# Order of the stores and of the key and value loads in part 1 of a memory-attention and SwiGLU kernel

## The chip, the core and the metric

The kernel runs on one core of a Trainium2 chip. The core has a matrix engine (PE, with its weight loads shown as PEld), a vector engine (DVE), a scalar engine (ACT), a general engine (POOL) and a sync engine (SP) whose queue issues the DMAs here. The metric is the device time of one launch in microseconds; lower is better. The time before is the median of three runs.

## The reference

Inputs: `q`, `k`, `v` of shape (8 batches, 8 heads, 576, 64), `phi` of shape (8, 8, 576, 32), and float64 weights `w_gate`, `w_val` (512 x 1536), `w_out` (1536 x 512) and `rms_g` (512).

```python
a = exp(phi - max(phi, axis=2));  a = a / (sum(a, axis=2) + 1e-9)      # softmax over the 576 positions
k_m = einsum('bhsm,bhsd->bhmd', a, k)                                  # 32 memory slots per head
v_m = einsum('bhsm,bhsd->bhmd', a, v)
attn = softmax(q @ k_m^T / 8)                                          # 576 x 32
x = (attn @ v_m) as 4608 tokens x 512
xn = x / sqrt(mean(x*x) + 1e-6) * rms_g
out = (silu(xn @ w_gate) * (xn @ w_val)) @ w_out                       # 4608 x 512
```

## The kernel before

Part 1 makes, for each batch b, the small matrices k_m and v_m, and for the first four batches also the attention weights. Part 2 is the gated network, in 48 steps `i` (two passes over 12 slices of the 1536 hidden columns, with two pairs of batches in each pass); into its first pass the attention of the other four batches is woven (`attend_steps`, `x2`).

Part 1 for one batch b: `load_phi` loads phi, `prep` takes its maximum and exponential into `e_bd` (lines 562 to 605) and adds some of its chunks on POOL into `es` (L617, L619; how many is `ESN[b]`). `load_kv(b, hp)` loads k and v of one pair of heads. `kv_steps(b)` has six chunks of matmuls (`kvp`, L636): the first three, the first half, need head pairs 0 and 1, the last three, the second half, need head pairs 2 and 3. Then come `sums` (matmuls with a column of ones, L651; `es` shortens them), `post1` (DVE, L659 to L668), `turn` (PE, L680), `post2` (ACT, and `vg` on POOL at L701), `self_products` (L710) and `post3` (`gram`, L719). For batches 4 to 7 `store` writes `vg` to `vg_dram` (L726) and, for 5 and 7, `gram` to `gram_dram` (L729); part 2 reads them back (`vgl<-vgd`, L1096, and `gb<-gd`, L199).

The key and value tiles of batches 2, 5 and 7 share the four buffers of the tag `kv`; those of 0, 3, 1, 4 and 6 lie in places that part 2 uses later (`kv_0x`, `kv_1x`). A load into a buffer waits on SP for the last reader of the tile that was there.

The float64 weights arrive as raw words (`raw`, two buffers) and are split into float32 parts by `convert` on DVE, ACT and POOL (L389 to L453); the results of slices are also written to DRAM (`wd<-wh`, `wd<-wl`, L464, and `od`, L459) and read back in the second pass by `reload` (L477). The first two slices (n = 0 and 1) are converted in part 1.

`x_steps` turns and normalises the attention weights of a pair of batches: `tp`, `xp`, then the chain `m`, `rinv` on DVE (L296 to L313), `rp` on PE (L230), `at` on DVE (L238), `ath` and `atl` (L258, L259).

Order. All steps of a part go into a list `ev` of (time, function) pairs, the times being in the planner's units, from the table `PRM`; the list is sorted and the functions are called in that order. The framework's scheduler then walks a modelled time line: of the instructions that its model holds to be ready, the earliest in the list goes first. So an instruction that waits, by the model, can be passed by a later one. On the chip each engine and the SP queue run what they got strictly in order. `load` ties each load behind the one issued before it (`issue_after`), so loads stay in the order of the list among themselves; stores and part 2's transfers have no such tie. The time of a key and value load in the list is

```python
ev.append((K_AT[b] + PRM["KD"][b * HP + hp], lambda b=b, hp=hp: load_kv(b, hp)))
```

which gives 101.115 for head pair 0 of batch 7 (167.28 - 66.165), and 109.651, 107.591, 113.281 and 111.017 for head pairs 0 to 3 of batch 5 (121.436 less the four values). The raw weights of slice 0 have 111.332 (`CV`).

Of the kernel before, what the change touches and what calls it, by code (L numbers as in the profile page):

```python
# [8 lines left out]
F32 = mybir.dt.float32  # L9
# [9 lines left out]
XTTR = True  # L19
WB = 4  # L20
PRM = dict(
    DS=150,
    KB=4,
    QB=3,
    K_AT=[13.363, 15.05, 40.982, 64.708, 100.72, 121.436, 147.13, 167.28],
    KP=0.88,
    POST=[-0.317, -0.206, 4.032, 7.881, 15.383, 23.226],
    P1=4.084,
    PREP=[4.511, 5.867, 6.271, 6.307, 20.4],
    PD=[1.603, 10.918, 5.724, 18.42, 6.909, 0.895],  # L30
    EXP=[-9.517, 14.262, 1.741, 4.567, 14.552, 4.082],
    ES=1.541,
    PH=[9.097, 16.192, 41.396, 73.222, 103.794, 133.428],
# [30 lines left out]
    O=[0.116, 0.297, 0.452, 0.514, 0.874, 0.991, 1.365, 1.487, 1.518],
    PRE=[-0.635, 0.045, 0.27, 1.342, 2.044, 2.566],
    PRE0=[-0.813, 0.784, 1.109, 1.622, 2.25, 2.293],
    PI=0.13,
    PSW=[1.981, 2.035, 1.951, 2.415, 3.159, 3.803],
    SU=[1.877, 3.104, 5.776, 6.56, 9.726, 12.211, 13.413, 15.536],
    AO=[0.214, 0.237, 0.237, 0.276, 0.397, 0.423, 0.543, 0.581, 0.621, 0.621, 0.621, 0.819, 1.065, 1.397],  # L70
    XB=[17.199, 22.761],
    XS=[0.1086, 0.0359],
    XM=[22.138, 25.161],
    XN=[-0.302, -0.244, -0.092, 0.028, 0.161, 0.484, 0.518, 0.593, 0.603],
    LV=[20.282, 20.03, 20.406, 21.652],
# [26 lines left out]
def kernel(  # L102
# [25 lines left out]
    nc = tc.nc  # L128
# [3 lines left out]
    HP = H // 2  # L132
# [6 lines left out]
    G = 2  # L139
# [190 lines left out]
    issued = []  # L330
# [4 lines left out]
            issued.append(nc.sync.dma_start(out, in_).ins)  # L335
# [42 lines left out]
    def convert(kind, n):  # L378

        d = {}  # L380
        nm = f"{kind}_{n}"
        V = nc.vector

        def s0():
            d["raw"] = t = raw.pop((kind, n))
            hw = t[:, :, 1]
            d["ex"] = ex = wp[0].tile([P, 512], I32, tag="ex", name=f"ex{nm}")
            with behind():
                V.tensor_scalar(out=ex, in0=hw, scalar1=0x7FF00000, scalar2=None, op0=ALU.bitwise_and)  # L389
# [9 lines left out]

        def s1():  # L400
            ex = d["ex"]
            if not ((kind < 2 and n < 2 and PRM["CA"]) or ((kind == 2 or n >= 2) and PRM["CB"])):
# [7 lines left out]

        def s2():
            d["m"] = m = wp[0].tile([P, 512], I32, tag="mi", name=f"mi{nm}")
            with behind():
                V.tensor_scalar(
                    out=m, in0=d["raw"][:, :, 1], scalar1=0xFFFFF, scalar2=None, op0=ALU.bitwise_and
                )
            mf = m.bitcast(F32)
            with behind():
                V.scalar_tensor_tensor(  # L419
                    out=mf, in0=d["raw"].bitcast(U32)[:, :, 0], scalar=2.0 ** -32, in1=m,  # L420
                    op0=ALU.mult, op1=ALU.add,
                )

        def s3():
            mf = d["m"].bitcast(F32)
            nc.scalar.activation(mf, mf, AF.Copy, scale=2.0 ** -20, bias=1.0)  # L426
            if kind < 2 and n < 2:
                d["w"] = wp[0].tile([P, 512], F32, tag="w", name=f"w{nm}")
            else:
                d["w"] = sb.tile([P, 512], F32, tag="w2", name=f"w{nm}", bufs=WB)  # L430

        def s4():
            m, ex = d["m"].bitcast(F32), d["ex"].bitcast(F32)
            on_pool = kind == 2 or n >= 2 or PRM["CE"][n] & (1 << kind)
            (nc.gpsimd if on_pool else V).tensor_tensor(out=d["w"], in0=m, in1=ex, op=ALU.mult)  # L435

        def s5():
            w = d["w"]
            if kind == 2:
                dh = wp[1].tile([P, 512], F32R, tag="oh", name=f"oh{n}", bufs=2)  # L440
                dl = wp[1].tile([P, 512], F32R, tag="ol", name=f"ol{n}", bufs=2)
                wosplit[n] = dh, dl
                src = w
            else:
                if kind == 0:
                    wsplit[n] = (
                        wp[n % 2].tile([P, HP, 2, P], F32R, tag="wh", name=f"wh{n}"),
                        wp[n % 2].tile([P, HP, 2, P], F32R, tag="wl", name=f"wl{n}"),
                    )
                dh, dl = (x[:, :, kind, :] for x in wsplit[n])  # L450
                src = w.rearrange("p (hp f) -> p hp f", hp=HP)
            nc.scalar.copy(dh, src)
            nc.gpsimd.tensor_tensor(out=dl, in0=src, in1=dh.bitcast(F32), op=ALU.subtract)  # L453

        def s6():

            if kind == 2:
                for a, t in enumerate(wosplit[n]):
                    nc.sync.dma_start(o_dram[n][:, a], t.bitcast(F32))  # L459
            elif kind == 1:  # L460
                for a, t in enumerate(wsplit[n]):
                    for h in range(2):
                        r = 64 * (h ^ a)
                        nc.sync.dma_start(w_dram[n][r:r + 64, h], t[64 * h:64 * h + 64].bitcast(F32))  # L464
# [15 lines left out]
    with ExitStack() as c1:  # L480
# [33 lines left out]
        st = {}  # L514
# [110 lines left out]
        def kv_steps(b):  # L625
# [97 lines left out]
                    split_v(b, st.pop(("vg", b)))  # L723

            def store():
                nc.sync.dma_start(vg_dram[b], st.pop(("vg", b)))  # L726
# [544 lines left out]
```

## Time and profile before

| what | value |
|---|---|
| time, median of 3 runs | 876.38 us (875.77 to 877.84) |
| time of the profiled execution | 876.4 us |
| its span, first to last instruction | 874.6 us |
| PE busy | 826.1 us (94%) |
| DVE, ACT, POOL busy | 541.1, 398.4, 315.3 us |
| mean granted PE clock | 0.982 |
| part 2's first matmuls (`vp`, L981) | 133.6 us after the start |

Rows of a timeline give start, duration, engine, line, operation and tiles, how many instructions are merged, and in brackets the idle time before them with what ended it. Rows of a table by windows give, for each stretch, its length and then busy time (and count) of PE, PEld, DVE, ACT and POOL, the granted PE clock (1.00 is full), the DMA engines' busy share and GB/s. Rows of the waits give the total, how many, and the longest. Matmul ends are modelled, so back-to-back matmuls overlap in the rows; their pace is the merged duration over the count. A float32 matmul appears as two rows.

### The profile page before, as it was taken

Reading aid. Unit: us, or ns where it says so; the run is one execution under the profiler, and the core shown is the slowest. Engines: PE = TensorE matmul, PEld = TensorE weight load, DVE = VectorE, ACT = ScalarE, POOL = GpSimd, SP = SyncE. Lnnn points to the kernel's source line nnn. Section 1 sums busy time; section 2 is a strip of 40 time slices with the busy share of each in tenths; the row PEclk is TensorE's granted clock in tenths of the full one; section 3 lists DMA queues with packets and bytes.
Section 4 is the critical chain, followed back from the end, with each engine's and each line's share of the span. In section 5 each row is a group of like instructions: output and inputs, shape, how many; then the busy total and the mean of one; then the engine's idle time right before and its main releaser. Section 6 shows DMA issues by size and latency. Waiting matters only on the chain.

```text
span 874.6 us, 16472 instructions
## 1 busy us (share of the span) xinstructions
PE 826.1 (94%) x6191; PEld 737.7 (84%) x6191; DVE 541.1 (62%) x985; ACT 398.4 (46%) x712; POOL 315.3 (36%) x268
## 2 busy tenths in 40 slices
PE   4998798989999999999999999989999999999997
PEld 4887777979988988978989977968999998999996
DVE  6679666878569888798889637402444444444434
ACT  3666336767655556646555413334322323232220
POOL 2475425644443553543534612302211212122120
PEclk9999797999999999999999999999999999999999
DMA  8992916553343453532543455755645546453437
GB/s 324 364 388 60 329 62 155 138 151 113 125 120 103 130 153 100 159 113 97 149 137 117 142 133 112 199 154 133 175 92 164 137 123 175 107 144 80 97 97 168
DMA packets 110246, 131.64 MB, mean 151 GB/s; under 512 B 45140, under 2 KB 74840, under 8 KB 110168
## 3 DMA queue, kind: packets, MB, share of 16 engines
q1 hardware_dynamic: 110168, 130.60, 52.2%
q8 instruction: 49, 0.80, 0.4%
q14 instruction: 29, 0.24, 0.1%
HBM read 73.93 MB, written 31.46 MB: 120 GB/s over the span
## 4 chain that ended last, share of the span: by engine, by line
PE 71%; DVE 11%; DMA 5%; issue 4%; ACT 4%; POOL 3%; SPq 2%; POOLq 0%; ACTq 0%; DVEq 0%
PE po L1064 28%; PE pg L1017 14%; PE pv L1017 14%; PE vp L981 3%; PE vq L931 3%; PE kvp L636 2%; DMA q<-in_q_dram 1%; DVE ex L389 1%; POOL w L435 1%; PE kvp L651 1%; DVE mi L419 1%; DVE acc L1072 1%; POOL hl L1045 1%; DVE ex L392 1%; DVE xl L994 1%
## 5 line engine op out<-in xcount | busy, mean ns | idle before, releaser
L1045 POOL TENSOR_TENSOR hl<-hf,hh 128x512 fp32r<-128x512 f32 (+1 forms) x86 | 126.3, 1471 | 280.9 <-ACT hh L1044 278.7
L1072 DVE TENSOR_TENSOR acc<-po,acc 128x512 f32<-128x512 f32 x180 | 123.2, 688 | 121.2 <-PE po L1064 120.2
L1064 PE MATMUL po<-oh,hh 128*128 128x512 f32 x387 | 155.8, 405 | 12.0 <-DVE acc L1072 4.0
L1064 PE MATMUL po<-ol,hh 128*128 128x512 f32 x387 | 153.8, 397 | 2.1 <-DMA ol<-od 2.1
L1064 PE MATMUL po<-oh,hl 128*128 128x512 f32 x387 | 153.3, 396 | 0.0
L1026 DVE TENSOR_TENSOR hf<-pv,sg 128x256 f32<-128x256 f32 x192 | 84.7, 452 | 101.1 <-PE pv L1017 52.7
L1025 ACT ACTIVATE sg<-pg 128x256 f32<-128x256 f32 x192 | 76.8, 410 | 129.1 <-PE pg L1017 121.4
L1064 PEld LDWEIGHTS po<-oh,hh 128*128 128x128 f32 x387 | 72.8, 189 | 27.4 <-DVE acc L1072 6.2
L1017 PE MATMUL pg<-ath,xh 128*128 128x320 f32 (+1 forms) x384 | 87.4, 301 | 4.6 <-ACT xh L993 4.4
L1017 PE MATMUL pg<-ath,xl 128*128 128x320 f32 (+1 forms) x384 | 86.4, 298 | 1.0 <-DMA xl<-sl 1.0
L1064 PEld LDWEIGHTS po<-oh,hl 128*128 128x128 f32 x387 | 73.2, 189 | 16.6
L1017 PE MATMUL pv<-ath,xl 128*128 128x320 f32 (+1 forms) x384 | 86.1, 297 | 0.0
L1017 PE MATMUL pv<-ath,xh 128*128 128x320 f32 (+1 forms) x384 | 85.7, 299 | 0.2 <-DVE hf L1026 0.2
L1017 PE MATMUL pg<-atl,xh 128*128 128x320 f32 (+1 forms) x384 | 84.7, 296 | 0.0
L1017 PE MATMUL pv<-atl,xh 128*128 128x320 f32 (+1 forms) x384 | 84.3, 297 | 0.0
L1044 ACT CAST hh<-hf 128x512 fp32r<-128x512 f32 (+1 forms) x86 | 57.4, 672 | 57.4 <-DVE hf L1026 41.0
L1064 PEld LDWEIGHTS po<-ol,hh 128*128 128x128 f32 x387 | 73.3, 189 | 11.9 <-DMA ol<-od 2.9
L435 POOL TENSOR_TENSOR w<-mi,ex 128x512 f32<-128x512 f32 x35 | 45.1, 1289 | 95.2 <-ACT mi L426 65.4
L1017 PEld LDWEIGHTS pg<-ath,xh 128*128 128x128 f32 x384 | 64.5, 189 | 10.0 <-ACT xh L993 5.2
L994 DVE TENSOR_TENSOR xl<-vp,xh 64x1024 fp32r<-64x1024 f32 x48 | 58.5, 1218 | 21.5 <-ACT xh L993 20.8
L1017 PEld LDWEIGHTS pg<-ath,xl 128*128 128x128 f32 x384 | 64.3, 190 | 4.1 <-issue 1.4
L1017 PEld LDWEIGHTS pv<-ath,xh 128*128 128x128 f32 x384 | 63.3, 190 | 3.3 <-PE pg L1017 0.4
(150 smaller groups left out, 1525.0 us busy)
## 6 DMA issues: line engine op xcount, KB each, us to landing
xh<-sh SPq DMA_DIRECT2D x192, 64.0 KB, 2.1
xl<-sl SPq DMA_DIRECT2D x192, 64.0 KB, 2.0
out_dram<-acc SPq DMA_DIRECT2D x72, 128.0 KB, 2.4
raw<-in_moe_w_gate_dram SPq DMA_DIRECT2D x12, 512.0 KB, 4.1
raw<-in_moe_w_val_dram SPq DMA_DIRECT2D x12, 512.0 KB, 3.8
wd<-wh SPq DMA_DIRECT2D x24, 256.0 KB, 3.2
wd<-wl SPq DMA_DIRECT2D x24, 256.0 KB, 3.7
raw<-in_moe_w_out_dram SPq DMA_DIRECT2D x12, 512.0 KB, 3.6
```

Of the source, the lines that this page charges most:

```text
L435: (nc.gpsimd if on_pool else V).tensor_tensor(out=d["w"], in0=m, in1=ex, op=ALU.mult)
L636: nc.tensor.matmul(kvp[64 * par:64 * par + 64, cc, 0:128], e_bd[j][:, hp, c, :], st["kv", b, hp][:, :, 64 * c:64 * c + 64], start=(c == 0) ...
L931: nc.tensor.matmul(vp[:, h, e, :], vall[a][:, cc, k:k + 4, :].rearrange("p q m -> p (q m)"), w, start=(a == 0), stop=(a == 1),)
L981: nc.tensor.matmul(vp[:, cc, e, :], lhs(l), r[:, 2 * cc + e, :], start=(n == 0), stop=(n == 2),)
L994: urgent.append(nc.vector.tensor_tensor(out=xl[rows], in0=src, in1=xh[rows].bitcast(F32), op=ALU.subtract).ins)
L1017: nc.tensor.matmul(pt[:, :N], l[cc][:, b, half * P:half * P + P], r[:, cc, b, t0:t0 + n, :].rearrange("p t x -> p (t x)"), start=(m == 0), ...
L1025: nc.scalar.activation(sg[:, :N], pg[:, :N], AF.Silu)
L1026: urgent.append(nc.vector.tensor_tensor(out=hf[:, :, b, :], in0=pv[:, :N].rearrange("p (t x) -> p t x", x=64), in1=sg[:, :N].rearrange("p ...
L1044: nc.scalar.copy(hh, hv)
L1045: nc.gpsimd.tensor_tensor(out=hl, in0=hv, in1=hh.bitcast(F32), op=ALU.subtract)
L1064: nc.tensor.matmul(po, l[:, tt, :], r, start=(m == 0), stop=(m == 5))
L1072: nc.vector.tensor_tensor(out=accs[key], in0=po, in1=accs[key], op=ALU.add).ins
```

## The change

`store_behind` ties a store behind the last load handed out so far. It is used for the stores of `vg` and `gram` (L726, L729) and for the stores of the converted slices 0 and 1 (L464). With a new number `LK` of 150, no key or value load has a time above 149.9 in the list, and no store of `vg` or `gram` one below 150. Most of the other numbers of `PRM` are new as well. Of the diff, the table is cut to the entries that are discussed later and some neighbours:

```diff
-    DS=150,
+    LK=150,
+    DS=154.273,
-    K_AT=[13.363, 15.05, 40.982, 64.708, 100.72, 121.436, 147.13, 167.28],
-    KP=0.88,
+    K_AT=[13.363, 15.05, 40.982, 64.708, 100.72, 121.436, 147.13, 167.903],
+    KP=0.914,
...
-    KD=[-15.069, -115.131, -42.204, -7.345, -6.094, -15.243, -0.175, -2.835, -28.265, -16.354, -17.024,
+    KD=[-15.069, -115.131, -42.204, -7.345, -6.094, -15.243, -0.175, -2.835, -29.404, -16.354, -17.024,
         -8.311, -12.025, -12.235, -27.337, -21.619, -22.801, -22.01, -23.715, -24.999, -11.785, -13.845,
-        -8.155, -10.419, -16.375, -22.685, -11.543, -19.501, -66.165, -9.755, -3.349, -20.028],
+        -8.155, -10.419, -16.375, -22.685, -11.543, -19.501, -20, -9.755, -3.349, -20.028],
...
-    QE=[4, 0],
-    CE=[3, 2],
-    XE=[12, 11, 29, 21],
-    ESN=[2, 3, 2, 0, 3, 1, 1, 1],
+    QE=[0, 0],
+    CE=[3, 0],
+    XE=[12, 11, 23, 29],
+    ESN=[2, 3, 2, 2, 3, 1, 1, 1],
...
-    VD=[29.86, 23.48, 21.637, 34.098],
+    VD=[29.894, 23.48, 16.936, 31.545],
...
-    RL=[-1.906, -3.752, -5.714],
-    RW=[1.932, 0.552],
+    RL=[-1.906, -3.412, -5.53],
+    RW=[1.622, 0.859],
...
+    def store_behind(out, in_):
+
+        with tc.issue_after(issued[-1]):
+            nc.sync.dma_start(out, in_)
...
-                        nc.sync.dma_start(w_dram[n][r:r + 64, h], t[64 * h:64 * h + 64].bitcast(F32))
+                        (store_behind if n < 2 else nc.sync.dma_start)(
+                            w_dram[n][r:r + 64, h], t[64 * h:64 * h + 64].bitcast(F32)
+                        )
...
             def store():
-                nc.sync.dma_start(vg_dram[b], st.pop(("vg", b)))
+                store_behind(vg_dram[b], st.pop(("vg", b)))
                 if j:
                     pr = b // 2
-                    nc.sync.dma_start(gram_dram[pr], gram[pr])
+                    store_behind(gram_dram[pr], gram[pr])
...
-                ev.append((K_AT[b] + 6 * PRM["KP"] + PRM["POST"][5] + PRM["VD"][b - 2 * G], store))
+                ev.append((max(K_AT[b] + 6 * PRM["KP"] + PRM["POST"][5] + PRM["VD"][b - 2 * G], PRM["LK"]), store))
...
-                    ev.append((K_AT[b] + PRM["KD"][b * HP + hp], lambda b=b, hp=hp: load_kv(b, hp)))
+                    ev.append((min(K_AT[b] + PRM["KD"][b * HP + hp], PRM["LK"] - 0.1), lambda b=b, hp=hp: load_kv(b, hp)))
```

`ESN[3]` of 2 instead of 0 lets POOL add two pairs of chunks of batch 3 ahead of its sums. `CE`, `QE` and `XE` say for single operations which engine takes them: the product of slice 1's second half goes from POOL to DVE, the last copies of the first four turned queries from DVE to ACT, and of the copies in `x_steps` for the later pairs one goes from DVE to ACT and one changes place. The other entries of the table that are not shown shift times in the list by mostly under half a unit in part 2 and by up to a few units in part 1.

More of the change, by code (lines that the diff above doesn't have):

```diff
@@ L21 @@
 PRM = dict(
-    DS=150,
+    LK=150,
+    DS=154.273,
     KB=4,
     QB=3,
-    K_AT=[13.363, 15.05, 40.982, 64.708, 100.72, 121.436, 147.13, 167.28],
-    KP=0.88,
[L27 to L33, printed above, removed]
+    K_AT=[13.363, 15.05, 40.982, 64.708, 100.72, 121.436, 147.13, 167.903],
+    KP=0.914,
+    POST=[0.041, 0.041, 3.361, 8.581, 15.173, 23.226],
+    P1=4.425,
+    PREP=[4.511, 6.478, 6.478, 6.478, 20.4],
+    PD=[1.603, 10.918, 5.603, 17.822, 6.909, 0.895],
+    EXP=[-7.764, 14.262, 1.692, 4.567, 14.552, 4.761],
+    ES=1.262,
+    PH=[9.097, 16.336, 41.396, 73.222, 103.794, 133.428],
     S_AT=[32.949, 48.182, 51.299, 66.888, 103.621, 110.401, 116.081, 122.952],
-    KD=[-15.069, -115.131, -42.204, -7.345, -6.094, -15.243, -0.175, -2.835, -28.265, -16.354, -17.024,
+    KD=[-15.069, -115.131, -42.204, -7.345, -6.094, -15.243, -0.175, -2.835, -29.404, -16.354, -17.024,
         -8.311, -12.025, -12.235, -27.337, -21.619, -22.801, -22.01, -23.715, -24.999, -11.785, -13.845,
-        -8.155, -10.419, -16.375, -22.685, -11.543, -19.501, -66.165, -9.755, -3.349, -20.028],
-    QD=[7.122, 5.589, 2.612, 8.893, 23.53, 19.934, 25.06, 15.038],
-    PD0=1.045,
+        -8.155, -10.419, -16.375, -22.685, -11.543, -19.501, -20, -9.755, -3.349, -20.028],
+    QD=[9.78, 5.589, 2.612, 12.908, 23.53, 19.934, 25.06, 15.038],
+    PD0=0.952,
     QL=3.761,
-    OL=3.513,
-    QO=[-1.164, 3.407, -1.815, -0.482, 0.012, 2.591],
-    SO=[7.743, 14.98, 18.206, 24.112],
+    OL=3.483,
+    QO=[-0.964, 4.247, -1.615, 1.156, 0.212, 3.193],
+    SO=[7.875, 14.417, 17.251, 24.624],
     X_AT=[100.536, 150.686],
-    XP=1.796,
+    XP=2.099,
     LAG=0.891,
@@ L49 @@
     CV2=160.133,
-    CP2=1.09,
-    QE=[4, 0],
-    CE=[3, 2],
-    XE=[12, 11, 29, 21],
-    ESN=[2, 3, 2, 0, 3, 1, 1, 1],
+    CP2=1.098,
+    QE=[0, 0],
+    CE=[3, 0],
+    XE=[12, 11, 23, 29],
+    ESN=[2, 3, 2, 2, 3, 1, 1, 1],
     SUM=[2, 2, 1, 0, 0, 1, 2, 1],
@@ L59 @@
     RS=6.461,
-    RP=0.555,
-    GV=[0.232, 0.246, 0.274, 0.752, 0.884, 1.089],
+    RP=0.036,
+    GV=[0.232, 0.246, 0.295, 0.762, 0.884, 1.143],
     VW=[-0.104, -0.023, 0.07],
     VW0=0.373,
[L64 to L70, printed above, removed]
-    XB=[17.199, 22.761],
[L72 to L75, printed above, removed]
-    VD=[29.86, 23.48, 21.637, 34.098],
-    U=[[-1.581, -1.578, -1.37, -1.197, -0.96, -0.96], [-1.522, -1.522, -1.12, -1.12, -1.036, -0.964], [-1.618,
-        -1.5, -1.335, -1.003, -1.003, -0.071]],
-    RL=[-1.906, -3.752, -5.714],
-    RW=[1.932, 0.552],
+    O=[0.116, 0.266, 0.452, 0.514, 0.874, 0.991, 1.365, 1.487, 1.518],
+    PRE=[-0.635, 0.045, 0.28, 1.342, 2.044, 2.566],
+    PRE0=[-0.813, 0.786, 1.109, 1.622, 2.25, 2.437],
+    PI=0.14,
+    PSW=[1.697, 2.033, 1.739, 2.203, 2.947, 3.543],
+    SU=[1.877, 3.104, 5.776, 6.56, 9.726, 12.952, 13.928, 15.536],
+    AO=[0.214, 0.215, 0.237, 0.276, 0.397, 0.423, 0.543, 0.581, 0.621, 0.621, 0.621, 0.819, 1.069, 1.397],
+    XB=[17.199, 22.761],
+    XS=[0.1086, 0.034],
+    XM=[22.138, 25.107],
+    XN=[-0.264, -0.206, -0.075, 0.066, 0.199, 0.522, 0.635, 0.635, 0.641],
+    LV=[20.329, 20.215, 20.555, 21.814],
+    VD=[29.894, 23.48, 16.936, 31.545],
+    U=[[-1.358, -1.358, -1.358, -1.197, -0.96, -0.832], [-1.522, -1.522, -1.12, -1.12, -1.036, -1.036],
+        [-1.54, -1.422, -1.257, -0.925, -0.925, 0.007]],
+    RL=[-1.906, -3.412, -5.53],
+    RW=[1.622, 0.859],
     CB=1,
```

## The prediction

> **What bounds the kernel now.** I read the busy times by window first, to see where PE is not full. (Columns: window, its length, busy time and count of PE, PEld, DVE, ACT, POOL, then granted clock, DMA share, GB/s.)
>
> ```profile
> 61.00:85.50 24.50, 22.78 (x344) 18.36 (x341) 23.15 (x56) 16.17 (x30) 11.15 (x11) 1.00 0.31 107
> 85.50:92.70 7.20, 1.84 (x11) 1.07 (x10) 5.21 (x17) 3.98 (x6) 4.87 (x9) 0.77 0.94 248
> 92.70:100.00 7.30, 7.26 (x99) 7.08 (x100) 2.35 (x2) 1.31 (x3) 1.42 (x2) 0.73 1.06 398
> 100.00:112.70 12.70, 11.22 (x183) 10.08 (x181) 11.77 (x27) 5.58 (x12) 7.68 (x9) 0.88 0.76 276
> 139.80:540.00 400.20, 386.20 (x2632) 346.75 (x2633) 310.52 (x526) 224.96 (x387) 177.49 (x137) 1.00 0.46 129
> 540.00:600.00 60.00, 55.99 (x327) 49.24 (x326) 17.12 (x30) 23.58 (x47) 16.72 (x13) 0.97 0.59 153
> 600.00:875.00 275.00, 268.93 (x1608) 242.76 (x1607) 116.65 (x200) 78.35 (x154) 54.94 (x39) 1.00 0.52 131
> ```
>
> Part 2 is PE's: it idles 14.0 us of 400 in the first pass, 4.0 around 570 and 6.1 later. Part 1 has one hole: from 85.5 to 92.7 PE works 1.84 of 7.2 us, while DVE, full before (23.15 of 24.5), has a little work and then none. The chain of waits says what ended it:
>
> ```profile
> 86.23 0.85 SPq L335
> 87.12 5.57 DMA kv<-in_v_dram
> 92.74 3.62 PE kvp L636 x33
> ```
>
> The chain runs through a key and value load that SP issued late. Why late is in SP's timeline, read against the list's times:
>
> ```profile
> 53.08 0.45 SPq L335 DMA_DIRECT2D kv<-in_k_dram  x1
> ...
> 58.69 0.33 SPq L335 DMA_DIRECT2D kv<-in_k_dram  x1
> ...
> 61.81 0.38 SPq L335 DMA_DIRECT2D raw<-in_moe_w_val_dram  x1
> 78.14 0.34 SPq L726 DMA_DIRECT2D vgd<-vg  x1
> 84.19 1.15 SPq L464 DMA_DIRECT2D wd<-wh  x2
> 85.60 0.45 SPq L464 DMA_DIRECT2D wd<-wl  x1
> 86.14 0.94 SPq L335 DMA_DIRECT2D kv<-in_k_dram  x1
> ```
>
> Loads go in the order of the list. By its times the four from 53.08 to 58.69 (two are left out) are batch 7's head pair 0 (101.115), then batch 5's 1, 0 and 3; the raw weights (111.332) follow, and batch 5's head pair 2 (113.281) is the one at 86.14. The tag has four buffers, and the early tile of batch 7 holds one that batch 5 needs. PE and DVE show the loop:
>
> ```profile
> 58.67 2.19 PE L636 MATMUL kvp<-kv_0x,e_bd 128*64 128x128 f32 x36
> ...
> 83.12 2.40 PE L636 MATMUL kvp<-kv,e_bd 128*64 128x128 f32 x38
> ...
> 89.36 0.47 PE L755 MATMUL qtp<-ident,qr 128*128 128x128 f32 x1 [1.82 <-DVE phi L595]
> 92.74 3.73 PE L636 MATMUL kvp<-kv,e_bd 128*64 128x128 f32 x33 [2.90 <-DMA kv<-in_v_dram]
> ...
> 96.70 1.09 PE L230 MATMUL rp<-ident,rinv 128*128 128x128 f32 x8
> ```
>
> ```profile
> 90.91 0.11 DVE L313 SCALAR_TENSOR_TENSOR rinv<-u,rinv 128x9 f32<-128x9 f32 x1
> 97.39 2.35 DVE L238 TENSOR_TENSOR at<-at,rp 128x1024 f32<-128x1024 f32 x2 [6.37 <-PE rp L230]
> 100.39 0.17 DVE L659 TENSOR_SCALAR kvp<-kvp 128x2 f32<-128x2 f32 x1 [0.65 <-PE kvp L651]
> ...
> 101.11 0.42 DVE L238 TENSOR_TENSOR at<-at,rp 128x256 f32<-128x256 f32 x1 [0.34 <-PE rp L230]
> ```
>
> The first half of batch 5 (36 rows, and 2 of head pair 3) ends at 85.5. Only then is a buffer free for head pair 2, whose v lands at 92.69 and is waited for. The `rp` turns stand behind it on PE, and DVE, done with `rinv` at 91.02, idles 6.37 us for them. After that DVE is full to 112.7 (11.77 of 12.7), so what it starts late is late to the end.
>
> **The change part by part.** The sum goes against the profiled execution's 876.4 us (span 874.6, 1.8 outside), which is the median of the runs shown (876.38).
>
> *Batch 7's head pair 0 behind batch 5.* Its time becomes 147.903 (167.903 - 20). Batch 5's four loads then take the four buffers and are issued by about 62.5, behind the raw weights at 61.81: some 20 us ahead of 83.12. What is late next? If PE keeps its order, the second half follows the turn that ends at 89.83. At the full pace (2.19/36 = 0.061 us a row) 33 rows take 2.0 instead of 3.73: they end at 91.84 instead of 96.47, and DVE starts at 92.8 instead of 97.39, 4.6 us earlier. If the new order puts the second half straight behind the first, it ends near 87.7 and the limit is `rinv` at 91.02: with the 0.69 from `rp` to DVE (96.70 to 97.39) DVE starts at 91.7, 5.7 us earlier. I take 5.4, nearer to the second, because a tile that is there by 83 no longer makes the planner push the second half back. Most that this place can give is all the idle time of DVE here, 6.37 + 0.65 + 0.34 = 7.4; least is nothing, if the order keeps the second half late. All later work of part 1 hangs on DVE or on PE behind it, and part 2 starts when part 1 has ended, so the gain is passed on.
>
> *Stores behind loads.* The store at 78.14 held the queue until then, as the waits of the SP queue say (total, times, longest):
>
> ```profile
> SPq L726 <- POOL vg L701: 28.2, 3, 15.5
> ```
>
> That looks large, but the next load could not go before 85.5 for want of a buffer: the stores cost it the stretch from 85.5 to 86.14, some 0.6 us, contained above. Once that load has its buffer, batch 6's eight loads and phi 7 are no longer behind it and the queue, and go from 62 on. They were not waited for before, so I book nothing. At the queue's head batch 7's loads then wait for batch 5's halves (85.5 and about 88), and tied behind them are the stores of batch 4's `vg` and slice 0, which move from 78 to 86 into about 88 to 100; raw slice 1's second half stands behind the loads too. Nobody needs these stores soon: the first that is read back is `gram`, at 123.27, and `vg` has two buffers. Cost 0; bound: up to 5.2 us if that read comes late, which ACT is shown waiting for once (125.35, idle 5.18).
>
> ```profile
> 123.27 1.22 SPq L199 DMA_DIRECT2D gb<-gd  x2
> 125.35 0.62 ACT L452 CAST wh<-w 128x512 fp32r<-128x512 f32 x1 [5.18 <-DMA gb<-gd]
> 53.30 3.37 PE L651 MATMUL kvp<-ones,e_bd 128*64 128x1 f32 x66
> 54.37 1.27 POOL L617 TENSOR_TENSOR es<-e_bd 128x512 f32<-128x512 f32 x1
> 128.76 1.26 POOL L435 TENSOR_TENSOR w<-mi,ex 128x512 f32<-128x512 f32 x1
> ```
>
> *`ESN[3]`.* Batch 3's sums fall from nine terms to seven: 16 of 72 rows at 3.37/66 = 0.05 us, 0.8 us of PE. POOL gets two adds of about 1.27 us ahead of them. I take half the gain, 0.4; ends 0.8 gained and 2.5 lost (both adds waited for).
>
> *`CE`, `QE`, `XE`.* One product leaves POOL (1.26) for DVE, and small copies go to ACT. They lie where DVE or POOL wait anyway; 0, ends 1 us each way.
>
> *The refitted order elsewhere.* No row shows it. The first pass has 14.0 us of PE idle that an order could win, so at best perhaps 5; at worst a new stall like the one around 570 (4.0 us). I take 0.
>
> Sum: 876.4 - 5.4 - 0.4 = 870.6.
>
> One rule is set against the rows here. In the windows the clock falls twice, once behind the hole and once without one:
>
> ```profile
> 94.00:96.00 2.00, 2.00 (x24) 2.00 (x22) 0.00 (x0) 0.00 (x0) 0.00 (x0) 0.50 1.04 403
> 100.00:102.00 2.00, 2.00 (x29) 1.66 (x29) 1.21 (x6) 1.40 (x4) 2.00 (x3) 0.50 1.08 399
> ```
>
> The first is in the sum (33 rows in 3.73 instead of 2.0). The second stands right behind the one-column sums with PE full, and since the sums stay, I leave its cost where it is. The Trainium skill (TensorE: Matmul & The Clock Gate, "What's actually happening") puts the half clock down to an idle window of about 3.4 us. By that rule alone the second fall would be an echo of the hole and vanish with it, an estimated 1 us more gained (half of the 2 us row), 869.6. The row without a gap ahead of it speaks for the other reading.
>
> **The rivals.** *More is won:* the refit also takes some 5 of the first pass's 14.0 idle us, or DVE gets all 7.4: 863 to 866.5. Against it: those gaps are many and small, and the pass is 97% full.
>
> *The hole closes and opens elsewhere:* DVE is full from 61 to 91, so if the refit brings more conversion work into it ahead of `rinv`, or leaves the second half late, the 5.4 is lost again: 875 to 877.5. For it: DVE's 23.15 of 24.5. Against: the work was the same amount before. That the change does not do what it says belongs here.
>
> *Slower:* `reload` of `w_out` in the second pass. `RW`'s second number puts it 0.307 step later for five groups.
>
> ```profile
> 611.53 0.36 SPq L477 DMA_DIRECT2D oh<-od  x1
> 723.52 0.40 PE L1064 MATMUL po<-oh,hx 128*128 128x512 f32 x1
> 724.51 0.53 SPq L477 DMA_DIRECT2D oh<-od  x1
> 731.12 0.70 PE L1064 MATMUL po<-oh,hh 128*128 128x512 f32 x2 [1.09 <-DMA oh<-od]
> ```
>
> From 611.53 to 724.51 are eight steps, 14.1 us each, so 4.3 us later. One of the five is waited for already (1.09). If SP's order really puts transfers ahead of them, PE waits up to 4.3 us five times: 870.6 + 21.5 = 892 at worst, and 881 with half of it. It decides above 1.2 us for each group (5.8/5). Against it: this reload waits for its buffer (the last reader is the `po` at 723.52), which the list's time does not move.
>
> **How the numbers follow.** This kernel's measurement can tell about 0.2%, 1.75 us. The forecast (867 to 874.5) has 0.58, more won 0.14, the hole elsewhere 0.14, slower 0.14. Faster takes the first two and a little of the third, 0.74; same 0.12; slower 0.14. The range reaches from 864.5, into the first rival, to 877, past the third case, leaving out about 2 in 10. The forecast's own range is 867 to 874.5: 7.4 with 1.6 of refit at the low end, about 2 us of gain at the other.
>
> **What the profile after would show.** Part 2 began so, in the chain:
>
> ```profile
> 133.59 2.88 PE vp L981 x12
> ```
>
> The profile after would show four `kv` loads for batch 5 between 53 and 64 and no load of the tag between there and 85; batch 6's loads from 62 on, in place of the empty stretch to 84; no wait for `kv<-in_v_dram` near 87; the `at` of L238 at 91 to 93; part 2's first `vp` near 128; then part 2's length as before within 4 us. The prediction is wrong if `vp` comes at 133, or if it comes at 128 and part 2 is longer, most likely at the `oh` and `ol` reloads.

## The result and the profile after

| | before | after |
|---|---|---|
| median of 13 runs each | 877.88 us (875.04 to 884.11) | 873.23 us (870.47 to 874.70) |
| ratio to before, 95% interval | 1 | 0.9933 (0.9911 to 0.9954) |
| profiled execution, span | 876.4, 874.6 us | 870.47, 868.7 us |
| mean granted PE clock | 0.982 | 0.98 |

The kernel is faster by 0.67% (0.46 to 0.89%), which is 5.9 us, close to the 5.8 us that were forecast; the medians lie 4.7 us apart. Executions that took over 1.5% longer than the fastest of the same kernel are left out of all ratios. The time came out, but not from the place that the forecast named. Lines of the changed kernel are 8 higher than those of before in the functions used here (`kvp` L644, sums L659, `at` L239 by one, `vp` L989, `po` L1072, `acc` L1080).

The busy times by window first (columns as before):

```profile
61.00:85.50 24.50, 17.84 (x254) 14.02 (x254) 23.12 (x52) 14.79 (x27) 12.40 (x14) 0.94 0.59 209
85.50:92.70 7.20, 7.20 (x85) 6.58 (x85) 7.03 (x18) 4.71 (x9) 4.05 (x3) 0.73 0.10 19
92.70:100.00 7.30, 7.30 (x114) 6.67 (x110) 5.37 (x16) 2.28 (x4) 1.92 (x2) 0.77 0.99 342
100.00:112.70 12.70, 7.93 (x141) 7.55 (x141) 8.49 (x18) 5.57 (x10) 8.19 (x9) 0.89 0.55 185
540.00:600.00 60.00, 56.27 (x336) 49.54 (x335) 16.79 (x31) 24.51 (x50) 17.24 (x13) 1.00 0.61 155
```

From 85.5 on PE has no hole any more (7.20 of 7.20, was 1.84). But the hole has only moved: the window ahead has lost 4.9 us of PE (22.78 to 17.84), and the one from 100 to 112.7 another 3.3 (11.22 to 7.93). SP's timeline shows that the loads did what they were meant to:

```profile
52.54 0.33 SPq L336 DMA_DIRECT2D kv<-in_k_dram  x1
...
59.39 0.34 SPq L336 DMA_DIRECT2D kv<-in_v_dram  x1
...
66.18 0.38 SPq L336 DMA_DIRECT2D phi<-in_phi_dram  x1
71.78 0.38 SPq L336 DMA_DIRECT2D raw<-in_moe_w_gate_dram  x1
90.99 0.33 SPq L336 DMA_DIRECT2D kv<-in_k_dram  x1
...
95.43 0.42 SPq L336 DMA_DIRECT2D kv<-in_v_dram  x1
95.95 0.38 SPq L342 DMA_DIRECT2D vgd<-vg  x1
96.42 1.15 SPq L342 DMA_DIRECT2D wd<-wh  x2
...
99.84 0.95 SPq L336 DMA_DIRECT2D raw<-in_moe_w_val_dram  x1
```

Batch 5's four loads go from 52.54 to 59.39, batch 6's from 60.19, and nothing of the tag until batch 7's at 90.99. No instruction waits for `kv<-in_v_dram` near 87 any more. But more came forward than that: batch 7's phi and the first half of slice 1's raw weights, at 66.18 and 71.78 now, stood behind the blocked load before:

```profile
91.86 0.38 SPq L335 DMA_DIRECT2D phi<-in_phi_dram  x1
...
94.18 0.38 SPq L335 DMA_DIRECT2D raw<-in_moe_w_gate_dram  x1
```

What PE waits for instead:

```profile
84.73 1.97 PE L763 MATMUL qtp<-ident,qr 128*128 128x128 f32 x8 [4.42 <-DVE phi L603]
87.54 2.35 PE L644 MATMUL kvp<-kv,e_bd 128*64 128x128 f32 x22
90.07 2.94 PE L644 MATMUL kvp<-kv,e_bd 128*64 128x128 f32 x49
95.44 1.33 PE L231 MATMUL rp<-ident,rinv 128*128 128x128 f32 x8
112.11 1.12 PE L211 MATMUL tp<-ident,a 128*128 128x128 f32 x4 [4.77 <-POOL a L826]
```

Before, the first half of batch 5 ran at 83.12. Now eight of the `qtp` turns stand ahead of all 72 rows, and they wait 4.42 us for the subtraction from batch 6's phi on DVE, the reader of `mr` (presumably of the bank that the turns take). The first 22 rows then take 0.107 us each (2.35/22), the later 49 0.060; the granted clock of the window is 0.73. `rp` stands behind the 72 rows and their sums and comes at 95.44. DVE's timeline says what it did meanwhile:

```profile
81.28 2.13 DVE L570 TENSOR_REDUCE mc<-phi 128x128 f32<-128x1152 f32 x1
83.33 1.34 DVE L603 TENSOR_TENSOR phi<-phi,mr 128x1152 f32<-128x1152 f32 x1
86.15 1.63 DVE L425 SCALAR_TENSOR_TENSOR mi<-raw,mi 128x512 f32<-128x512 uint32 x1
93.88 0.17 DVE L314 SCALAR_TENSOR_TENSOR rinv<-u,rinv 128x9 f32<-128x9 f32 x1
95.54 0.17 DVE L667 TENSOR_SCALAR kvp<-kvp 128x2 f32<-128x2 f32 x1 [1.49 <-PE kvp L659]
96.12 1.22 DVE L239 TENSOR_TENSOR at<-at,rp 128x1024 f32<-128x1024 f32 x1 [0.20 <-PE rp L231]
106.76 0.43 DVE L395 TENSOR_SCALAR ex<-raw 128x512 int32<-128x512 int32 x1 [2.29 <-DMA raw<-in_moe_w_val_dram]
```

The 2.13 us maximum of batch 7's phi (`mc`) now runs ahead of batch 6's subtraction; then slice 1's conversion runs ahead of `rinv`, which ends at 94.05 instead of 91.02. Before, neither could run here: their loads were issued only at 91.86 and 94.18, and `mc` ran at 102.31. The wait that ends last before `at` is PE's, though: behind `rinv` DVE idles another 1.49 us for the sums, and the chain of waits goes from `mc` over the subtraction to the turns, the rows, the sums and `rp`. `at` follows `rp`, at 96.12, 1.3 us earlier than before (97.39), not the 5.4 that were booked. Then DVE waits 2.29 us for the raw weights that SP issued at 99.84, behind batch 7's loads and the tied stores, and PE behind it 4.77. The chain of waits shows that this wait is on the path, and when part 2 starts:

```profile
99.84 6.89 DMA raw<-in_moe_w_val_dram
...
133.00 2.87 PE vp L989 x12
```

133.00 against 133.59 before: part 1 gave 0.6 us of the 5.9 between the spans. The rest is part 2's. I compared the start of every fourth of the 192 `sg` instructions, counted from the first. Up to the 57th they agree with before within 0.7 us; then, a few aside that changed places with a neighbour, the 61st is 1.5 earlier, the 73rd 2.7, the 97th 4.8, and from the 157th on all are 5.3 earlier. (In between, these starts also move because work of the attention was put later.) One stretch with a part of the gain, first before, then after:

```profile
360.00:400.00 40.00, 37.22 (x269) 32.36 (x268) 34.02 (x51) 22.09 (x37) 20.88 (x16) 1.00 0.53 161
```

```profile
360.00:400.00 40.00, 39.07 (x302) 34.88 (x301) 33.30 (x57) 25.84 (x41) 18.68 (x14) 1.00 0.56 154
```

In the same 40 us PE works 1.85 us more and runs 33 rows more. Before, the longest hole there was that of an add to `acc`, which frees the bank that the next `po` product needs. PE and DVE of before:

```profile
378.51 0.50 PE L1064 MATMUL po<-oh,hh 128*128 128x512 f32 x1 [1.11 <-DVE acc L1072]
```

```profile
376.04 0.69 DVE L419 SCALAR_TENSOR_TENSOR mi<-raw,mi 128x512 f32<-128x512 uint32 x1
376.65 1.21 DVE L994 TENSOR_TENSOR xl<-vp,xh 64x1024 fp32r<-64x1024 f32 x1
377.78 1.27 DVE L1072 TENSOR_TENSOR acc<-po,acc 128x512 f32<-128x512 f32 x2
```

DVE converts and splits first and adds second, and PE waits 1.11 us; the changed kernel has no such wait in this stretch. From the first `vp` to the end of the span PE idles 27.1 us before and 23.1 after, so 4.0 of the 5.3 us are idle time: 1.85 of them in this stretch, and 1.09 the wait for a reload of `w_out` (731.12 before), which after does not have. The rest can be the clock: from 540 to 600 it is granted at 0.97 before and at 1.00 after, by estimate 1.8 us (0.03 of 60).

### The profile page after: what moved, and what is told of

Read it like the earlier page. It is cut to its first block, busy times and chain, and to the rows that moved or that the text cites. A ratio compares the mean times of both kernels' runs of the same rounds, so it can differ in the third digit from the quotient of the medians.

```text
span 868.7 us, 16412 instructions
## 1 busy us (share of the span) xinstructions
PE 822.5 (95%) x6159; PEld 736.0 (85%) x6159; DVE 544.2 (63%) x981; ACT 399.3 (46%) x717; POOL 317.5 (37%) x269
## 4 chain that ended last, share of the span: by engine, by line
PE 75%; DVE 11%; DMA 3%; ACT 3%; issue 3%; SPq 2%; POOL 2%; DVEq 0%; POOLq 0%; ACTq 0%
PE po L1072 29%; PE pg L1025 15%; PE pv L1025 15%; PE vp L989 3%; PE kvp L644 3%; PE vq L939 3%; DVE mi L420 1%; DVE ex L395 1%; DVE xl L1002 1%; PE kvp L659 1%; PE xp L273 1%; PE qtp L763 1%; DVE mi L425 1%; SPq L970 1%; DVE ex L398 1%
## 5 line engine op out<-in xcount | busy, mean ns | idle before, releaser
L1080 DVE TENSOR_TENSOR acc<-po,acc 128x512 f32<-128x512 f32 x180 | 123.6, 688 | 135.8 <-PE po L1072 135.2
L1072 PE MATMUL po<-oh,hh 128*128 128x512 f32 x387 | 154.6, 401 | 6.0 <-DVE ex L1163 1.8
L1072 PE MATMUL po<-ol,hh 128*128 128x512 f32 x387 | 152.9, 395 | 1.5 <-DMA ol<-od 1.5
L1072 PE MATMUL po<-oh,hl 128*128 128x512 f32 x387 | 152.8, 395 | 0.0
L1072 PEld LDWEIGHTS po<-oh,hh 128*128 128x128 f32 x387 | 72.8, 188 | 19.1 <-ACT acc L1077 2.4
L1072 PEld LDWEIGHTS po<-oh,hl 128*128 128x128 f32 x387 | 72.8, 188 | 16.4
L1025 PE MATMUL pg<-atl,xh 128*128 128x320 f32 (+1 forms) x384 | 85.5, 297 | 0.0
L1072 PEld LDWEIGHTS po<-ol,hh 128*128 128x128 f32 x387 | 72.9, 188 | 11.0 <-DMA ol<-od 2.0
L441 POOL TENSOR_TENSOR w<-mi,ex 128x512 f32<-128x512 f32 x34 | 43.9, 1290 | 93.9 <-ACT mi L432 70.1
L1025 PEld LDWEIGHTS pg<-ath,xh 128*128 128x128 f32 x384 | 64.9, 190 | 11.3 <-ACT xh L1001 5.5
L1002 DVE TENSOR_TENSOR xl<-vp,xh 64x1024 fp32r<-64x1024 f32 x48 | 58.5, 1220 | 21.5 <-ACT xh L1001 20.8
```

Source lines behind the costliest of these rows:

```text
L1002: urgent.append(nc.vector.tensor_tensor(out=xl[rows], in0=src, in1=xh[rows].bitcast(F32), op=ALU.subtract).ins)
L1025: nc.tensor.matmul(pt[:, :N], l[cc][:, b, half * P:half * P + P], r[:, cc, b, t0:t0 + n, :].rearrange("p t x -> p (t x)"), start=(m == 0), ...
L1072: nc.tensor.matmul(po, l[:, tt, :], r, start=(m == 0), stop=(m == 5))
L1080: nc.vector.tensor_tensor(out=accs[key], in0=po, in1=accs[key], op=ALU.add).ins
```

## The experiments

Three marks cut part 1 in each profiled execution: the start of the first `tp` of `x_steps` for the first pair on PE, of the first `at` on DVE, of the second pair's first `tp` on PE, and of part 2's first `vp`. They are read from the records of the instructions. The last column runs from the first `vp` to the last `sg`. All in us.

| kernel | ratio, 95% interval | to first tp | tp to at | at to 2nd tp | to vp | tp to vp | part 2 |
|---|---|---|---|---|---|---|---|
| before | 1 | 66.3 | 31.1 | 15.4 | 20.8 | 67.2 | 714.7 |
| after | 0.9933 (0.9911 to 0.9954) | 63.3 | 32.9 | 16.0 | 20.8 | 69.7 | 709.4 |
| p2_of_before | 0.9994 (0.9972 to 1.0015) | 63.1 | 32.9 | 15.9 | 20.9 | 69.6 | 713.9 |
| p2_of_after | 0.9953 (0.9928 to 0.9977) | 73.1 | 31.6 | 15.0 | 21.3 | 67.9 | 710.0 |
| su_alone | 0.9968 (0.9946 to 0.9990) | 68.6 | 31.0 | 15.1 | 21.1 | 67.1 | 710.4 |
| kd_alone | 1.0055 (1.0032 to 1.0078) | 66.8 | 34.8 | 14.5 | 23.9 | 73.2 | 713.2 |
| ties_alone | 1.0006 (0.9972 to 1.0041) | 70.6 | 28.3 | 17.4 | 24.2 | 69.8 | 713.7 |
| raw_ahead | 0.9939 (0.9913 to 0.9965) | 64.1 | 34.2 | 10.7 | 23.0 | 67.9 | 712.3 |
| raw_and_mc | 0.9886 (0.9839 to 0.9933) | 66.5 | 34.0 | 11.8 | 19.1 | 64.8 | 709.5 |
| mc_behind | 0.9973 (0.9955 to 0.9992) | 64.4 | 33.3 | 15.7 | 24.2 | 73.2 | 711.1 |
| hold | 0.9965 (0.9948 to 0.9982) | 66.8 | 33.3 | 14.5 | 23.1 | 70.9 | 710.5 |
| hold_no_mc | 0.9964 (0.9946 to 0.9982) | 68.0 | 32.7 | 14.5 | 24.0 | 71.2 | 710.5 |
| kv5_early | 0.9976 (0.9949 to 1.0002) | 64.9 | 36.8 | 6.6 | 26.7 | 70.1 | 708.2 |
| kv5_hold | 0.9940 (0.9916 to 0.9965) | 66.4 | 31.7 | 8.8 | 28.8 | 69.3 | 710.3 |

The third column is the one that chance moves most: with part 1 as before it was 66.3, 73.1 and 68.6 in three executions, so one execution says little about it. Each kernel was profiled once; the ratio rests on 4 to 13 timed runs of it, against runs of before made beside them.

**Which part gives the time?** The two kernels are each other's half.

```diff
# p2_of_before: the changed kernel with part 2's numbers set back
-    SU=[1.877, 3.104, 5.776, 6.56, 9.726, 12.952, 13.928, 15.536],
+    SU=[1.877, 3.104, 5.776, 6.56, 9.726, 12.211, 13.413, 15.536],
     # likewise XE[2:], GV, O, PRE, PRE0, PI, PSW, AO, XS, XM, XN, LV, U, RL, RW
# p2_of_after: before, with the same numbers from the changed kernel
```

> The changed kernel with part 2's numbers (GV, O, PRE, PRE0, PI, PSW, SU, AO, XS, XM, XN, LV, U, RL, RW, and XE for the later pairs) set back. Part 1 runs in the changed order, part 2 in the old one. Theory A, the gain is part 2's: the first vp near 133.0 and the whole time at that of before, ratio 0.998 to 1.001. Theory B, the gain comes from part 1's stores and loads and only shows in part 2: ratio 0.992 to 0.995.

> The kernel before with part 2's new numbers alone. Part 1 runs in the old order, with the late key and value load and the old place of the stores. Theory A: the first vp near 133.6 and the ratio 0.993 to 0.996 (some 4 to 5 us less). Theory B: ratio 0.998 to 1.001.

Part 1's changes alone, ties, loads and all, give nothing that can be measured (0.9994). Part 2's numbers alone give 0.9953, and the two ratios multiplied (0.9947) lie in the interval of the whole. The last column agrees: 713.2 to 714.7 us in the four kernels with part 2's old numbers, 708.2 to 712.3 in the nine with all its new ones, whatever part 1 was. The means are 713.9 and 710.2; 3.7 us apart is a safer figure for part 2 than the 5.3 between before and after alone, and nearer to the 0.47%, 4.1 us, of p2_of_after. The stretch from 360 to 400 with part 2's old numbers (p2_of_before), then with the new (p2_of_after):

```profile
360.00:400.00 40.00, 37.23 (x270) 32.38 (x269) 33.98 (x51) 22.08 (x37) 20.45 (x15) 1.00 0.52 155
```

```profile
360.00:400.00 40.00, 39.33 (x301) 35.43 (x301) 33.89 (x54) 26.95 (x45) 21.32 (x16) 1.00 0.57 155
```

The profiled execution of p2_of_after was one with a long start (73.1 to the first `tp`), so its span of 877.3 says nothing; the ratio does.

**Which numbers of part 2?**

```diff
# su_alone: before, and only
-    SU=[1.877, 3.104, 5.776, 6.56, 9.726, 12.211, 13.413, 15.536],
+    SU=[1.877, 3.104, 5.776, 6.56, 9.726, 12.952, 13.928, 15.536],
```

> The kernel before with two numbers changed: the start times SU of the sixth and seventh of the eight attention pieces woven into part 2's first pass, 12.211 to 12.952 and 13.413 to 13.928 steps. The first difference of the two traces in part 2 stands at step 13. Theory S, these two times carry the first pass's gain: from step 13 to step 24 some 3 to 5 us less, the whole time 0.994 to 0.997 of before. Rival T, the gain is spread over the many small numbers (GV, O, PRE, PSW): less than 1 us from step 13 on, ratio 0.998 to 1.001.

`SU` are the times at which the eight runs of `attend_steps` start in the list; two of them go 0.74 and 0.52 step later. That alone gives 0.9968 (2.8 us of 877.9), and in its profiled execution part 2 takes 710.4 instead of 714.7. PE between 360 and 400 is as full as after:

```profile
360.00:400.00 40.00, 39.06 (x290) 35.09 (x289) 33.61 (x57) 25.18 (x40) 20.07 (x16) 1.00 0.58 161
```

Two entries give 0.32 of the 0.47% by the ratios, and 4.3 of 5.3 us in the profiled executions; what the other numbers of part 2 add is within the intervals, and 710.4 is already the mean of the kernels with all the new numbers. That the adds to `acc` are what the two entries mend is shown for the stretch above alone; for the rest it stays open.

**The two edits that the change is named for, each alone.**

```diff
# kd_alone: before, and only batch 7's head pair 0
-    KD=[..., -66.165, -9.755, -3.349, -20.028]
+    KD=[..., -20, -9.755, -3.349, -20.028]
# ties_alone: before's numbers, with LK=150, store_behind and the two bounds on times
```

> The kernel before with one number changed: batch 7's head pair 0 loaded behind batch 5's (KD -66.165 to -20), no ties of the stores. Theory D, DVE's work binds the middle of part 1: the wait for kv<-in_v_dram near 87 goes, PE waits for DVE there instead, and the first vp comes within 1.5 us of 133.6. Theory of the prediction: vp near 128, ratio 0.993 to 0.995.

> The kernel before with the ties of the stores and the bounds at LK = 150 and all its old numbers: batch 7's head pair 0 keeps the early buffer. Both theories: the wait for batch 5's late load stays near 87 to 92 (its buffer, not the stores, holds it), the first vp within 1 us of 133.6, ratio 0.998 to 1.002. If the stores were what held the load, the load would be issued well before 85 and vp would come some 4 us earlier.

The step that carried the forecast, tried by itself, made the kernel slower by 0.55% (0.32 to 0.78%). Its loads came early as intended and no `kv` load was waited for, but part 1 was 6 us longer from `tp` to `vp` than before, with new waits for DVE; both theories had expected less. PE of kd_alone, then DVE:

```profile
85.92 1.12 PE L269 MATMUL xp<-gb,at 128*64 128x128 f32 x8 [2.89 <-DVE ssq L282]
96.00 0.35 PE L752 MATMUL qtp<-ident,qr 128*128 128x128 f32 x1 [1.26 <-DVE phi L592]
```

```profile
82.78 2.09 DVE L559 TENSOR_REDUCE mc<-phi 128x128 f32<-128x1152 f32 x1
94.61 1.34 DVE L592 TENSOR_TENSOR phi<-phi,mr 128x1152 f32<-128x1152 f32 x1
```

One number in the list reorders the whole neighbourhood, on DVE too: batch 7's phi goes out at 68.36, `mc` and slice 1's conversion (from 88.44) run ahead of batch 6's subtraction, and that ends at 95.95. In ties_alone, where the early tile keeps its buffer, phi goes out at 93.33 and `mc` runs at 103.46, both late as before. So the work that fills DVE came with the loads that this edit sets free.

The ties alone give no difference that the ratio can tell; their ten runs spread from 873.1 to 888.7 us, and the profiled one took 882.2. Its trace holds one thing that neither theory expected. The load still waits for its buffer (it is issued at 89.55, when the first half's rows end), but no store stands between the two, and PE does not wait for it any more:

```profile
93.58 0.38 PE L763 MATMUL qtp<-ident,qr 128*128 128x128 f32 x1 [1.82 <-DVE phi L603]
93.89 3.64 PE L644 MATMUL kvp<-kv,e_bd 128*64 128x128 f32 x33
```

`at` starts 28.3 us after `tp`, 2.8 sooner than before, which is about the 2.90 of that wait; the two stages behind it give back 5.4.

**The raw weights behind the tied stores.** In the changed kernel DVE waits 2.29 us for them.

```diff
# raw_ahead: the changed kernel, slice 1's second raw load at 150.05, ahead of batch 7's loads
-    LK=150,
+    LK=150.4,
-    ... min(K_AT[b] + PRM["KD"][b * HP + hp], PRM["LK"] - 0.1)
+    ... 150.2 + 0.01 * (hp ^ 1) if b == B - 1 else min(...)
-        ev += place(PRM["CV"], [PRM["CP"] * i for i in range(len(w))], w)
+        ev += place(PRM["CV"], [PRM["CP"] * i for i in range(len(w) - 1)] + [PRM["CP"] * 11.52], w)
```

> The changed kernel with the load of the second half of slice 1's raw weights moved ahead of batch 7's four key and value loads, and so ahead of the stores tied behind these (LK 150.4, batch 7's loads at 150.2 to 150.23, this load at 150.05). Theory W, the wait for that load (DVE idle 2.29 us at 106.76) ends part 1's chain: the wait goes and the first vp comes near 130.7 instead of 133.0, the time some 2 us below the changed kernel's. Theory D, DVE's work as a whole binds and an earlier conversion only stands in front of something else: the wait goes, another takes its place, and vp stays within 1 us of 133.

```diff
# raw_and_mc: raw_ahead, and batch 7's mc held behind batch 6's subtraction on DVE
+                with tc.issue_after(less[b - 1]) if b == B - 1 else nullcontext():
                     nc.vector.tensor_reduce(out=mc[:, :hp1 - hp0], ...)
```

> As raw_ahead, and batch 7's maximum (mc, 2.1 us on DVE) tied behind batch 6's subtraction (phi, L603 in the changed kernel), which it passed in the changed order while PE waited 4.42 us for that subtraction. Theory W: both stalls go, vp near 127 to 129, the time 4 to 6 us below the changed kernel's. Theory D: the PE wait at 84.7 shrinks by about 2 us, but the work comes back later on DVE and vp is not before 131.

raw_ahead takes the wait away and shortens the stage behind `at` from 16.0 to 10.7, but the last stage grows by 2.2 and the first by 1.3, and the time stays that of after, as Theory D had it. With the order of `mc` mended as well, PE's wait of 4.42 is 2.37, the last stage falls to 19.1, `tp` to `vp` is 4.8 us shorter than in after (`vp` itself, at 131.3, comes only 1.6 earlier, as the start was 3.2 longer), and the kernel reaches 868.3 us, 0.9886 of before (0.9839 to 0.9933, four runs): the best of all versions, faster than before; against after the intervals overlap.

**DVE's order alone.**

```diff
# mc_behind: the changed kernel, and only the tie of mc
# hold: mc_behind, and slice 1's conversions held back on DVE
+    def held(kind, n):
+        if (kind, n) == (0, 1):
+            return lambda: tc.issue_after(mark["at", 0])        # behind the first pair's third at
+        if (kind, n) == (1, 1):
+            return lambda: tc.issue_after(mark["kb", B - 2])    # behind batch 6's kb, vb
+        return behind_urgent
# hold_no_mc: hold without the tie of mc
```

> The changed kernel with batch 7's maximum tied behind batch 6's subtraction on DVE, and nothing else. Theory W, that passing of 2.1 us, on which PE waits 4.42 us, and the wait for the raw load are separate losses that add: vp near 131 here (131.3 with both mended), the time 1.5 to 2 us below the changed kernel's, ratio to before 0.991 to 0.993. Theory D: the work only moves on DVE, the wait for the raw load (2.29 us) stays or grows, vp 132 to 133.5, ratio 0.993 to 0.995.

> The changed kernel with three DVE pieces held in the places that they had before: batch 7's maximum behind batch 6's subtraction, the conversion of slice 1's first half (some 4.4 us of DVE) behind the third at multiplication of the first pair, that of its second half behind batch 6's kb and vb. Stages by marks (first tp on PE to the first at on DVE; from there to the first tp of the second pair; from there to the first vp): before 31.0, 15.4, 20.8, together 67.2 us; changed 32.9, 16.0, 20.8, together 69.7. Theory D, the hole was filled with DVE work that had been harmless later, and that this work now stands ahead of rinv: 27 to 28.5, 13.5 to 15.5, 20.8 to 21.5, together 62 to 65, and the time 5 to 7 us below the changed kernel's, ratio to before 0.985 to 0.989. Rival P, PE's own order binds the stretch: together 68 to 70, ratio 0.993 to 0.995.

> As hold, but batch 7's maximum passes as in the changed kernel; only the two conversions are held. Theory D: the first stage 29 to 30.5 us (2.1 us more than with the maximum held), together 64 to 67, ratio 0.987 to 0.991. Rival P: together 68 to 70.

None of the three is faster than after (0.9964 to 0.9973 against 0.9933), so the idea that DVE's order by itself held `at` back falls: `tp` to `at` stays at 32.7 to 33.3. In hold and hold_no_mc the conversions are out of the way, and DVE then waits 3.87 and 3.44 us for PE's sums, ahead of `at`; there PE's order holds it. DVE of hold:

```profile
99.50 0.17 DVE L679 TENSOR_SCALAR kvp<-kvp 128x2 f32<-128x2 f32 x1 [3.87 <-PE kvp L671]
```

In mc_behind the 4.42 us wait of PE goes down to 2.37, but POOL's `a` for the second pair is no earlier, and the boundary to part 2 has waits that after did not have (134.70; another of 1.14 at 136.96):

```profile
83.81 1.12 PE L766 MATMUL qtp<-ident,qr 128*128 128x128 f32 x4 [2.37 <-DVE phi L606]
113.44 1.97 PE L211 MATMUL tp<-ident,a 128*128 128x128 f32 x8 [4.86 <-POOL a L829]
134.70 0.69 PE L691 MATMUL kvt<-ident,kb 128*128 128x128 f32 x2 [1.06 <-DVE kb L679]
```

**PE's order too.**

```diff
# kv5_early: the changed kernel, batch 5's rows ahead of the qtp turns
-            ev += place(K_AT[b], [PRM["KP"] * i for i in range(6)], steps)
+            ev += place(K_AT[b] - (4.6 if b == 5 else 0), [PRM["KP"] * i for i in range(6)], steps)
# kv5_hold: hold, with the same line
```

> The changed kernel with one edit: the six steps of batch 5's key-value product stand 4.6 units earlier in the list (K_AT[5] - 4.6), so that PE has all 72 rows of it ahead of the last two qtp turns of the row before; DVE's order is left as it is (batch 7's mc ahead of batch 6's phi, slice 1's conversion ahead of rinv). Theory J (both DVE's order and PE's order have to be mended before at can start earlier): only about 1.2 us can be won, since DVE is full until about 94: first tp to first at 31.5 us (32.85 in the changed kernel), first tp to first vp 68 to 69 us (69.7), ratio 0.991 to 0.994. Rival K (PE's order alone is what put the hole there): first tp to first at falls to 28 us or less, first tp to first vp to 65, ratio 0.988 or below. Rival L (no order of these two decides, another wait takes over): first tp to first vp 69.7 or more, ratio 0.993 to 0.998.

> As kv5_early, and DVE's order is mended as well: batch 7's mc is tied behind batch 6's phi subtraction, slice 1's conversions behind the first at (first half) and behind batch 6's kb and vb (second half). Theory J: at then starts right behind rp, first tp to first at 25.5 to 28 us, first at to the second pair's first tp about 14.5, from there to the first vp 21 to 23, together 62 to 65 us (69.7 in the changed kernel), ratio 0.986 to 0.990. Rival K (PE's order alone): like kv5_early within 1 us. Rival L: the first stage does get shorter, but the work that is held back is waited for later, as in the kernels with DVE's order alone: together 68 us or more, ratio 0.994 to 0.998.

Theory J falls, and so does K. In kv5_early the rows of batch 5 run from 78.9, and yet `at` starts 36.8 us after `tp`: DVE converts slice 1 first and has `rinv` only at 98.9. In kv5_hold the hole of PE before 92 is gone, DVE still has `rinv` only at 96.7, and the conversions that were held back are waited for afterwards. PE, then DVE, of kv5_hold:

```profile
106.68 0.45 PE L606 MATMUL mr<-ident,mb 128*128 128x128 f32 x1 [3.30 <-DVE mb L601]
```

```profile
104.59 1.55 DVE L434 SCALAR_TENSOR_TENSOR mi<-raw,mi 128x512 f32<-128x512 uint32 x1
```

That is what L said: the next wait takes over. The whole stage from `tp` to `vp` as one window each, of before, after, raw_and_mc and kv5_hold:

```profile
66.35:133.59 67.24, 58.27 (x806) 49.28 (x806) 51.85 (x141) 29.81 (x57) 28.15 (x31) 0.87 0.43 143
```

```profile
63.43:133.09 69.66, 58.07 (x806) 49.82 (x805) 54.42 (x140) 29.66 (x56) 27.55 (x30) 0.86 0.41 143
```

```profile
66.67:131.51 64.84, 56.97 (x806) 48.45 (x805) 53.14 (x140) 29.68 (x56) 27.55 (x30) 0.88 0.44 151
```

```profile
66.32:135.60 69.28, 59.83 (x805) 50.45 (x805) 55.75 (x142) 32.48 (x62) 30.93 (x31) 0.82 0.43 141
```

In these four the same rows take PE 57 to 60 us, and 8 to 12 us are idle; in the others that were tried PE takes up to 62 us, and 9 to 14 are idle. Which order would bring the idle time well below that stays open.

## Why the prediction was right, and where not

The prediction gave a sign of being wrong: `vp` at 133. It came at 133.0, and part 2 was shorter, so by that sign the mechanism failed, though the total fell into the range.

*Batch 7's head pair 0 behind batch 5 (-5.4).* The load half is right, line by line: four loads by 59.39, none of the tag until 90.99, no wait near 87. The failing step is the pair of orders that it reckoned with: that PE keeps its order, or puts the second half straight behind the first. It did neither: both halves went behind turns that wait for DVE. `at` came at 96.12 instead of 91 to 93, and counted from `tp` 1.8 us later than before (32.9 against 31.1). Behind that stands a sentence of the part on the stores: of the loads set free, phi 7 among them, it says that nobody had waited for them, and books nothing. Nobody waited, but they brought `mc` and a conversion into DVE some 21 us earlier. kd_alone prices the edit by itself at +0.55%. The rival "the hole closes and opens elsewhere" is what happened in part 1, nearly by the way it named: the work came into DVE ahead of `rinv`, but what it held up was, first, the subtraction that PE's turns wait for. Its answer to itself, that the work was the same amount before, missed that the work could come earlier.

*Stores behind loads (0).* The queue did as described: batch 7's loads wait at its head for batch 5, stores from 95.95 on. The late read of `gram` cost nothing. That the stores cost batch 5's load some 0.6 us was too little: in ties_alone PE's wait of 2.90 is gone with the buffer as late as before. And of the raw weights of slice 1, which the text put behind those loads as well, it did not ask who waits: 2.29 us of DVE on the path.

*`ESN[3]` (-0.4).* The count was wrong. With `n` of 2, `es` takes the place of six chunks, so nine terms fall to five, not seven: 40 rows instead of 72. The sums' windows, before and after:

```profile
53.20:56.80 3.60, 3.60 (x72) 1.00 1.04 407
```

```profile
51.80:53.90 2.10, 1.82 (x40) 1.00 1.04 409
```

1.8 us of PE less. Whether the start is shorter by it can't be told: the first `tp` came at 63.3 and 63.1 in the two executions with part 1 as changed and at 66.3 to 73.1 in three with it as before, but at 64.1 to 68.0 in the seven kernels that vary the changed one. What there was is given back between `tp` and `vp` (+2.5). p2_of_before, with both, is 0.9994.

*The refitted order elsewhere (0).* This is the term that was mis-sized: -5.3 us in the profiled executions, -0.47% (4.1 us) by p2_of_after, and most of it by two entries of `SU`. The 14.0 us of PE's idle time in the first pass were in the prediction, with "at best perhaps 5" beside them; the sum took 0 because no single row is large. The stall at 378 could have been read beforehand: an add to `acc` behind a conversion and a split on DVE, with softmax steps started in the same stretch.

*The rivals.* More won: its mechanism, a refit that takes idle time out of part 2, is what carried the result, without the other 5.4. Of the first pass's 14.0 idle us it took 2.6, not 5. `reload` later: did not occur; the wait of 1.09 at 731.12 is gone in after, and 540 to 600 has as much PE work as before (56.27 busy against 55.99).

*The clock.* The prediction left the second fall of the clock where it was, against the Trainium skill (TensorE: Matmul & The Clock Gate, "What's actually happening"), which puts the half clock down to an idle window. After, PE is full from 84.73 to 100, and the clock falls again behind the sums that end at 95.5:

```profile
96.00:98.00 2.00, 2.00 (x29) 1.67 (x29) 1.88 (x3) 0.62 (x2) 0.00 (x0) 0.54 1.03 346
```

That fits the other reading, but does not decide, since the hole was not gone but moved to 80.3 to 84.7. kv5_hold has no such hole, its longest wait of PE from 66 to 90.8 being 0.61 us, and its clock falls too, behind sums that run, with other matmuls between them, from 86.4 to 90.9:

```profile
84.00:90.80 6.80, 6.19 (x104) 5.60 (x101) 5.33 (x13) 5.77 (x9) 5.74 (x9) 1.00 0.95 319
90.80:94.20 3.40, 3.40 (x45) 3.00 (x44) 3.33 (x15) 0.00 (x0) 1.17 (x1) 0.50 1.00 368
```

So the traces here do not agree with an idle window as the only cause. Nor are sums enough: behind batch 3's, from 53.2 to 56.8 before, the granted clock stays at 1.00 to 64. What else it takes is open.

So the total was right by luck, by two errors that cancelled: 5.4 us booked where 0.6 came, 0 booked where 5.3 came, in the profiled executions.

## What to carry to other kernels

When a list of times is refitted along with an edit, the refit is a change of its own: swap each half of the numbers against the old ones before giving the edit the credit. A load moved ahead takes away its own wait, not the time, unless the engine that is full next to it (DVE here) has nothing else that can move into the gap; ask what the planner will put there, and begin with the loads that stood behind the one that was moved. And where a store or a load is tied to the end of a queue, follow every transfer behind it to its reader, not only the one that the edit is about.

## What was not expected of the hardware

The start of a launch varies: with the same part 1, the first `tp` came 66.3, 68.6 and 73.1 us after the start, while the stages behind it agree within 0.8 us (67.1 to 67.9 from `tp` to `vp`). So these first 70 us can make up to 6.8 us of the spread of 875 to 884 us between runs of before. Why they differ is open; the granted clock from 10 to 30 us was 0.77 and 0.55 by tens in the longest of the three, 1.00 and 0.83 in the shortest. And a 2 us reduction on DVE that swaps places with a 1.3 us subtraction showed up as a 4.42 us hole on PE (2.37 with the swap undone in mc_behind), because PE's order had the turns that need the latter ahead of 72 rows that were ready.
